# Pooled attention and a mixture of experts: another order of loads, products and copies while the first query tiles are prepared

## The chip, the cores and the metric

The kernel runs on one core of a Trainium2 chip. The metric is the device time of one execution in microseconds (us), as the median over runs. The engines named below are PE (TensorE: products, and transposes as products with an identity), PEld (its weight loads), DVE (VectorE), ACT (ScalarE), POOL (GpSimd) and SP (SyncE). ACT, SP and POOL also issue transfers, each into a queue of its own; those of POOL turn float32 into bf16 on the way where the tiles differ in type. Each engine works through its instructions in the order in which they were written, and waits for semaphores where an operand or a buffer isn't ready.

## The reference

```python
# 8 batches, 8 heads, 576 positions, head size 64
def _attn_ref(q, k, v):
    B, H, S, D = q.shape
    pool = 8
    Sp = S // pool                       # 72
    scale = 1.0 / np.sqrt(D)
    k_p = k.reshape(B, H, Sp, pool, D).mean(axis=3)
    v_p = v.reshape(B, H, Sp, pool, D).mean(axis=3)
    scores = scale * np.matmul(q, k_p.transpose(0, 1, 3, 2))
    scores = scores - np.max(scores, axis=-1, keepdims=True)
    attn = np.exp(scores)
    attn = attn / (np.sum(attn, axis=-1, keepdims=True) + 1e-09)
    return np.matmul(attn, v_p).astype(np.float32)

# x: the attention's output as 4608 tokens of 512; 4 experts, inner size 1024
def _moe_ref(x, domain_probs, w1, w2):
    p = domain_probs / (domain_probs.sum(-1, keepdims=True) + 1e-09)
    out = np.zeros((N, D), dtype=np.float32)
    for e in range(E):
        h = np.maximum(x @ w1[e], 0.0)
        out += p[:, e:e + 1] * (h @ w2[e])
    return out
```

## The kernel before

The 4608 tokens are 36 tiles of 128 (a tile has all 8 heads), and 4 tiles are a group of 512. For each tile the attention runs through a chain: turn the queries (`qT`), `scores`, `maxima` and `less` (subtract the maximum), `expo`, turn the probabilities (`attn_T`), and the context, which ends in `xT`, the group's tokens with the model dimension on partitions. For each group and each expert an up product with `w1` and a relu give `hs`, and a down product with `w2` is collected with the domain's probability into `acc`. The main loop at the end (`for s in range(NSTEP)`, 36 steps of 12 slots) runs the up products of step s + 1 between the down products of step s; the attention of later groups hangs on its slots by `plan`. The order of every engine's work is that of the program text; nothing is rescheduled.

What stands before that loop is written out by hand for the first group, tiles 0 to 3, all of batch 0. Its parts:

- **Loads.** The queries of tile c come by `load_q0(c, queue)` (L138) in float32 into `qf[c]`: tile 0 from ACT, tile 1 from SP, tiles 2 and 3 from POOL. The keys of batch 0 come from SP in three parts into `kf` (L146 a tail, L148 rows 0 to 1 and rows 2 to 3), in front of tile 1's queries; the domain probabilities `dpr` (L154) follow behind them. POOL waits for tile 0's queries by a copy of one element (`waited`, L171), and then issues values, w1 and w2 and tile 2's and 3's queries in the order of L172 to L189.
- **Queries of tiles 0 to 3.** `split_q(c)` casts them to bf16 on ACT (L597), `turn_q0(c)` turns them on PE by 16 products with the identity (L605), `take_q0(c)` copies the result to `qT` on ACT (L613).
- **Keys and values of batch 0.** `fold_keys0` adds each part's 8 rows on DVE (L636, L641), `turn_keys0` turns it on PE (L648), `take_keys0` copies it on DVE (L661). `sum_values0` adds the values on PE (L668), `spread_values0` spreads them on DVE (L677).
- **Tiles 0 and 1.** `sums_by_products` has the sums of the probabilities from PE (L689, then L694 and L696 on DVE); `context_rows` gives the context by rows (L419), scaled on DVE in two halves `x_sb` (L428); `turn_x` turns each half on PE (L703) and copies it to `xT` on ACT (L706). Tiles 2 and 3 use `normalise` and `context` (L449, copy L455).
- **Up product by tile.** `up_tile(s, i, starts)` (L482) runs 16 products for each of two halves of the inner dimension, each half into one PSUM buffer, and behind each a relu on ACT (L486).
- **Idle products.** `idle_products(n)` runs n products of zeros (L622) whose result nobody reads.

PSUM has pools: `ps_h` (two buffers: the up products' outputs, the turned keys, the sums of values, and `xT_ps`), `ps_t` (two: turned queries, turned probabilities, contexts), `ps_o` (two: down products, sums, idle products), `ps_s` (one: scores). A tile in a pool waits until the last reader of the buffer's former tile is done.

`scores(1)` and what comes until the loop over tiles 2 and 3 is the order that the diff edits (bottom of the listing). In it tile 2's cast stands right behind `attn_T(0)`, its turning ahead of `turn_x(0)`, and `scores(3)` behind the whole `down(0, 0)`.

Of the kernel before, what the change touches and what calls it, by code (L numbers as in the profile page):

```python
# [1 line left out]

# [6 lines left out]
ACT = mybir.ActivationFunctionType  # L10
ALU = mybir.AluOpType
AX = mybir.AxisListType
BF16 = mybir.dt.bfloat16
# [4 lines left out]
def kernel(  # L18
# [10 lines left out]
    nc = tc.nc  # L29
# [3 lines left out]
    P = nc.NUM_PARTITIONS  # L33
# [4 lines left out]
    FB = F // P  # L38
# [3 lines left out]
    TPG = G // P  # L42
# [21 lines left out]
    ps_h = ctx.enter_context(tc.tile_pool(name="ps_h", bufs=2, space=PS))  # L64
    ps_o = ctx.enter_context(tc.tile_pool(name="ps_o", bufs=2, space=PS))
    ps_s = ctx.enter_context(tc.tile_pool(name="ps_s", bufs=1, space=PS))
    ps_t = ctx.enter_context(tc.tile_pool(name="ps_t", bufs=2, space=PS))
# [25 lines left out]
    def segments(t0, n):  # L93
        segs = []
        t = t0
        while t < t0 + n:
            b = t // S
            end = min(t0 + n, (b + 1) * S)
            segs.append((b, t - b * S, end - t, t - t0))
            t = end  # L100
        return segs
# [33 lines left out]
    qf = [raw.tile([P, R, D], F32, name=f"qf{c}") for c in range(TPG)]  # L135

    def load_q0(c, queue):
        queue.dma_start(  # L138
            out=qf[c][:].rearrange("p r d -> p (r d)"),
            in_=q[0][:, c * P:(c + 1) * P, :].rearrange("h (c r) d -> c h (r d)", r=R),  # L140
        )
# [5 lines left out]
    for i in (0, 2):  # L147
        nc.sync.dma_start(  # L148
            out=kf[:, i:i + 2, :],
            in_=rows0[i * P:(i + 2) * P].rearrange("(i p) x -> p i x", p=P),  # L150
        )
    load_q0(1, nc.sync)
    dpr = const.tile([NT, P, E], F32, name="dpr")
    nc.sync.dma_start(out=dpr[:], in_=moe_domain_probs.rearrange("(t p) e -> t p e", p=P))  # L154

    still = const.tile([P, G], BF16, name="still")
    nc.vector.memset(still[:], 0.0)  # L157
# [5 lines left out]
    for sign, base in ((1, 0), (-1, SP - 1)):  # L163
        nc.gpsimd.affine_select(
            out=own[:], in_=own[:], compare_op=ALU.is_ge, fill=0.0,
# [159 lines left out]
    def scores(t):  # L325
        sc = ps_s.tile([P, 2, 512], F32, name="sc")
        for b, _, n, at in segments(t * P, P):
            for pair in range(NPAIR):
                nc.tensor.matmul(  # L329
                    sc[at:at + n, pair // 2, (pair % 2) * PW:(pair % 2 + 1) * PW],  # L330
                    lhsT=qT[t][:, pair, at:at + n],
                    rhs=kT[b][:].rearrange("x i p -> x (i p)")[:, pair * PW:(pair + 1) * PW],
                )
        scs[t] = sc
# [6 lines left out]
    def maxima(t):  # L341
        mxs[t] = soft.tile([P, 2, 4], F32, name="mx")
        nc.vector.reduce_max(out=mxs[t][:], in_=by_head(t), axis=AX.X)  # L343

    def less(t):
        st[t] = soft.tile([P, 2, 4, SP], F32, name="d_sb")
        nc.vector.tensor_tensor(  # L347
            out=st[t][:], in0=by_head(t),
            in1=mxs[t][:].unsqueeze(3).to_broadcast([P, 2, 4, SP]), op=ALU.subtract,
        )  # L350

    def less_max(t):
        maxima(t)
        less(t)
# [21 lines left out]
    def sums(t):  # L376
        e = st[t][:]
        if by_dma(t):
            e = attn[t % 2][:, 0:ROWS].rearrange("p (h j) -> p h j", j=SP)
        es = soft.tile([P, H], F32, name="es")  # L380
        nc.vector.reduce_sum(out=es[:], in_=e, axis=AX.X)  # L381
        nc.vector.tensor_scalar_add(out=es[:], in0=es[:], scalar1=1e-9)
        rss[t] = soft.tile([P, H], F32, name="rs")
        nc.vector.reciprocal(out=rss[t][:], in_=es[:])

    def normalise(t):
        sums(t)
        e_sb, rs = st[t], rss[t]
        nc.vector.scalar_tensor_tensor(
            out=attn[t % 2][:, 0:ROWS].rearrange("p (h j) -> p h j", j=SP),  # L390
            in0=e_sb[:], scalar=V_MEAN,
            in1=rs[:].unsqueeze(2).to_broadcast([P, H, SP]),
            op0=ALU.mult, op1=ALU.mult,
        )
# [63 lines left out]
    hs, accs = {}, {}  # L458
# [11 lines left out]
        nc.scalar.activation(out=hs[s][:, fb, :], in_=ps[:], func=ACT.Relu)  # L470


    def up_tile(s, i, starts=tuple(range(0, FB, TPG))):
        g, e = divmod(s, E)
        if s not in hs:
            hs[s] = hpool.tile([P, FB, G], BF16, name="h_sb")
        cols = slice(i * P, (i + 1) * P)
        for f0 in starts:
            ps = ps_h.tile([P, TPG, P], F32, tag="h", name="h_ps")
            for f in range(TPG):  # L480
                for kc in range(KC):
                    nc.tensor.matmul(  # L482
                        ps[:, f], lhsT=w1_sb[e][:, kc, (f0 + f) * P:(f0 + f + 1) * P],
                        rhs=xT[g][:, kc, cols], start=(kc == 0), stop=(kc == KC - 1),
                    )
            nc.scalar.activation(  # L486
                out=hs[s][:, f0:f0 + TPG, cols], in_=ps[:], func=ACT.Relu
            )

    o_ps = {}  # L490

    def down(s, i, f0=0, f1=FB):
        g, e = divmod(s, E)
        t = g * TPG + i
        if f0 == 0:
            o_ps[t] = ps_o.tile([P, DM], F32, name="o_ps")
        ps = o_ps[t]
        for fb in range(f0, f1):
            nc.tensor.matmul(  # L499
                ps[:], lhsT=hs[s][:, fb, i * P:(i + 1) * P], rhs=w2_sb[e][:, fb, :],  # L500
                start=(fb == 0), stop=(fb == FB - 1),
            )
# [76 lines left out]
    for g in range(2, NG):  # L579
        for i in range(TPG):  # L580
            t = g * TPG + i
# [14 lines left out]
    def split_q(c):  # L596
        nc.scalar.copy(out=qrow[c][:], in_=qf[c][:])  # L597


    def turn_q0(c):  # L600
        ps = ps_t.tile([P, R, NC, NPAIR], F32, tag="t", name="qT_ps")
        heads = ident[:].rearrange("x (c a z) -> x c a z", z=2, c=NC)
        for r in range(R):
            for z in range(2):
                nc.tensor.matmul(  # L605
                    ps[z * D:(z + 1) * D, r], lhsT=qrow[c][:, r], rhs=heads[:, :, :, z],
                    start=True, stop=True,
                )
        return ps

    def take_q0(c, ps):
        qT[c] = qtp.tile([P, NPAIR, P], BF16, name="qT")
        nc.scalar.copy(  # L613
            out=qT[c][:].rearrange("x a (c r) -> x a c r", r=R),
            in_=ps[:].rearrange("x r c a -> x a c r"),
        )


    def idle_products(n):
        ps = ps_o.tile([P, DM], F32, name="o_ps")  # L620
        for _ in range(n):
            nc.tensor.matmul(ps[:], lhsT=still[:, 0:P], rhs=still[:], start=True, stop=True)  # L622
# [8 lines left out]
    def fold_keys0(p1, i0, i1):  # L631
        rows = kraw[0][0:p1, i0:i1]
        src = kf[0:p1, i0:i1]
        for n in (4, 2):
            w = n * D
            nc.vector.tensor_add(  # L636
                out=rows[:, :, 0:w], in0=src[:, :, 0:w], in1=src[:, :, w:2 * w]
            )
            src = rows
        twice = [p1, i1 - i0, 2, D]  # L640
        nc.vector.tensor_tensor(  # L641
            out=kpad0[0:p1, i0:i1], in0=rows[:, :, 0:D].unsqueeze(2).to_broadcast(twice),
            in1=rows[:, :, D:2 * D].unsqueeze(2).to_broadcast(twice), op=ALU.add,
        )

    def turn_keys0(p1, i0, i1):
        for i in range(i0, i1):
            nc.tensor.transpose(  # L648
                kT_ps[:, i, 0:p1], kpad0[0:p1, i].rearrange("p z d -> p (z d)"),
                ident[0:p1, 0:p1],  # L650
            )
# [46 lines left out]
    def turn_x(t, halves):  # L698
        n = KC // 2
        for i in range(2):  # L700
            ps = ps_h.tile([P, n, P], BF16, tag="h", name="xT_ps")
            for kc in range(n):
                nc.tensor.transpose(  # L703
                    ps[:, kc], halves[i][:, kc * P:(kc + 1) * P], ident[:]
                )
            nc.scalar.copy(  # L706
                out=xT[0][:, i * n:(i + 1) * n, t * P:(t + 1) * P], in_=ps[:]
            )
        idle_products(1)
# [6 lines left out]
    take_q0(0, turn_q0(0))  # L716
    for part, n in (((TAIL, 4, 5), 3), ((P, 0, 2), 4), ((P, 2, 4), 3)):
        fold_keys0(*part)
        turn_keys0(*part)
        idle_products(n)  # L720
    take_keys0()
# [6 lines left out]
    spread_values0(sum_values0())  # L728
    scores(1)
    attn_T(0)  # L730
    split_q(2)
    maxima(1)
    idle_products(2)
    xT[0] = grp.tile([P, KC, G], BF16, name="xT")
    sums_by_products(0)
    x_sb = context_rows(0, 2)
    pt = turn_probs()
    qT_ps = turn_q0(2)
    idle_products(1)
    turn_x(0, x_sb)  # L740
    less(1)
    expo(1)
    take_q0(2, qT_ps)
    domain_probs(pt)
    up_tile(0, 0, (0,))
    attn_T(1, copy=nc.vector.tensor_copy)
    up_tile(0, 0, (TPG,))
    split_q(3)
    sums_by_products(1)
    x_sb = context_rows(1, 2)  # L750
    scores(2)
    idle_products(1)
    turn_x(1, x_sb)
    less_max(2)
    expo(2)
    up_tile(0, 1, (0,))
    take_q0(3, turn_q0(3))
    up_tile(0, 1, (TPG,))
    down(0, 0)
    scores(3)  # L760
    normalise(2)
    less_max(3)
    collect(0, 0)
# [20 lines left out]
    for s in range(NSTEP):  # L784
        for slot in range(SLOTS):
            part, i = slot % 3, slot // 3
# [41 lines left out]
```

## Time and profile before

| what | value |
|---|---|
| median of 3 runs | 550.18 us (549.75 to 551.51) |
| the profiled execution, its time | 550.72 us |
| the profiled execution, its span (first to last instruction) | 548.6 us |
| PE busy | 538.1 us, 98% of the span |
| ACT, DVE, POOL busy | 213.0, 263.8, 70.7 us |
| first up product of the main loop (L466) starts | 36.58 us |
| mean load on the 16 DMA engines, 18 to 38 us | over 1 (1.28), 204 GB/s |

A line of the timeline or the chain of waits has the start and the length in us, the engine and what ran. A group of instructions shows the output tile, an arrow and the inputs; `x16` is a count. A load's line in the list of issues has the median time from issue to landing, which for one issue is its own time. PE's busy time counts pipelined products, so a busy PE need not be one at its peak. Matmul starts are followed by the next in the array before they end, and the reader of a PSUM tile starts about 0.3 to 0.5 us behind the last product's start. Where a stretch of the span is shown, its columns are busy time and count for each engine, the granted clock of PE, the share of the DMA engines and GB/s.

### The profile page before, as it was taken

How to read it: one execution, taken by the hardware profiler on the slowest of the kernel's cores; microseconds unless marked ns; L12 is line 12 of the kernel's file. 1: busy time of each engine (PE TensorE's matmuls, PEld its weight loads, DVE VectorE, ACT ScalarE, POOL GpSimd, SP SyncE). 2: the span in 40 equal slices, each digit the busy share in tenths (PEclk: the TensorE clock that was granted, in tenths of full speed). 3: DMA queues.
4: the chain of work that ended last, by engine and by line, in shares of the span. 5: the costliest groups of instructions: out<-in, count | busy, mean ns of one | idle time of the engine just before them, and what ended most of it. 6: DMA issues, size and time to landing. Idle time of an engine off the chain costs nothing.

```text
span 548.6 us, 7422 instructions
## 1 busy us (share of the span) xinstructions
PE 538.1 (98%) x2945; PEld 262.7 (48%) x3000; DVE 263.8 (48%) x457; ACT 213.0 (39%) x356; POOL 70.7 (13%) x120
## 2 busy tenths in 40 slices
PE   8899999999999999999999999999999999999997
PEld 3664554444444444444444444444444444444444
DVE  5764847444744446544554444744474444422223
ACT  2554653333333333333333333333333333333330
POOL 6344101121111101012011100101010000000000
PEclk9999999999999999999999999999999999999999
DMA  9999935655646463366535642335333431111002
GB/s 207 219 203 196 201 43 129 83 76 83 124 67 78 77 121 75 49 85 103 99 53 78 81 108 39 54 41 110 51 53 42 85 65 31 23 38 39 0 1 76
DMA packets 110273, 46.43 MB, mean 85 GB/s; under 512 B 87548, under 2 KB 104764, under 8 KB 110240
## 3 DMA queue, kind: packets, MB, share of 16 engines
q0 software_dynamic: 51040, 21.96, 32.3%
q1 hardware_dynamic: 58912, 23.68, 17.9%
q8 instruction: 23, 0.38, 0.3%
q10 hardware_dynamic: 288, 0.33, 0.3%
q14 instruction: 10, 0.08, 0.1%
HBM read 45.16 MB, written 9.44 MB: 100 GB/s over the span
## 4 chain that ended last, share of the span: by engine, by line
PE 95%; DMA 2%; ACT 1%; issue 1%; POOL 1%; DVE 0%
PE o_ps L499 45%; PE h_ps L466 44%; DMA qf<-in_q_dram 2%; PE x_ps L419 2%; PE sc L329 2%; PE h_ps L482 1%; PE x_ps L449 0%; PE at_ps L403 0%; PE o_ps L531 0%; POOL vraw L80 0%; PE qT_ps L319 0%; ACT qrow L597 0%; ACT xT L706 0%; PE qT_ps L605 0%; DVE d_sb L347 0%
## 5 line engine op out<-in xcount | busy, mean ns | idle before, releaser
L470 ACT ACTIVATE h_sb<-h_ps 128x512 bf16<-128x512 f32 x280 | 167.1, 597 | 296.2 <-PE h_ps L466 292.0
L466 PE MATMUL h_ps<-xT,w 128*128 128x512 bf16 x1088 | 271.6, 379 | 1.5
L499 PE MATMUL o_ps<-w,h_sb 128*128 128x512 bf16 x1122 | 268.3, 379 | 1.3
L499 PEld LDWEIGHTS <-h_sb 128*128 128x128 bf16 x1144 | 111.6, 98 | 132.9
L514 DVE SCALAR_TENSOR_TENSOR acc<-o_ps,p_sb,acc 128x512 f32<-128x512 f32 x107 | 80.3, 750 | 179.5 <-PE o_ps L499 176.8
L466 PEld LDWEIGHTS <-w 128*128 128x128 bf16 x1120 | 106.0, 98 | 117.1
L510 DVE TENSOR_SCALAR acc<-o_ps,p_sb 128x512 f32<-128x512 f32 x36 | 27.0, 750 | 61.6 <-PE o_ps L499 61.6
L557 POOL COPY gated<-x_sb0of 1x1 bf16<-1x1 bf16 x28 | 7.8, 278 | 365.5 <-DVE x_sb0of L428 365.5
L108 POOL DMA_DIRECT2D qrow<-in_q_dram x36 | 30.4, 847 | 23.5 <-issue 7.7
L343 DVE TENSOR_REDUCE mx<-sc 128x8 f32<-128x576 f32 x36 | 27.2, 756 | 12.0 <-PE sc L329 12.0
L347 DVE TENSOR_TENSOR d_sb<-sc,mx 128x576 f32<-128x576 f32 x36 | 27.3, 757 | 1.2
L428 DVE SCALAR_TENSOR_TENSOR x_sb0of<-x_ps,rs 128x512 bf16<-128x512 f32 (+1 forms) x30 | 20.2, 674 | 12.4 <-PE x_ps L419 11.7
L360 ACT ACTIVATE attn<-d_sb 128x576 bf16<-128x576 f32 x30 | 20.5, 683 | 3.8 <-DVE d_sb L347 0.6
L381 DVE TENSOR_REDUCE es<-attn 128x8 f32<-128x576 bf16 x28 | 20.8, 744 | 0.0
L419 PEld LDWEIGHTS <-attnT 128*128 128x128 bf16 (+1 forms) x165 | 12.4, 100 | 7.2 <-issue 1.3
L329 PEld LDWEIGHTS <-qT 128*128 128x128 bf16 (+1 forms) x160 | 11.1, 100 | 8.7 <-issue 2.0
L419 PE MATMUL x_ps<-vbd,attnT 128*128 128x192 bf16 (+5 forms) x165 | 15.2, 231 | 0.0
L329 PE MATMUL sc<-kT,qT 128*128 128x144 bf16 (+1 forms) x160 | 15.0, 227 | 0.1
L622 PE MATMUL o_ps<-still 128*128 128x512 bf16 x30 | 10.4, 470 | 1.3 <-DVE still L157 1.3
L244 DVE TENSOR_TENSOR vraw<-vraw 128x1280 bf16<-128x1280 bf16 (+1 forms) x14 | 9.1, 653 | 0.2
L244 DVE TENSOR_TENSOR kraw<-kraw 128x1280 bf16<-128x1280 bf16 (+1 forms) x14 | 9.0, 641 | 0.2
L482 PE MATMUL h_ps<-xT,w 128*128 128x128 bf16 x128 | 8.4, 219 | 0.4 <-ACT xT L455 0.2
(86 smaller groups left out, 153.1 us busy)
## 6 DMA issues: line engine op xcount, KB each, us to landing
out_dram<-acc SPq DMA_DIRECT2D x35, 256.0 KB, 2.0
w<-in_moe_w_dram POOLq DMA_DIRECT2D x10, 512.0 KB, 14.1
kraw<-in_k_dram POOLq DMA_DIRECT2D x7, 512.0 KB, 7.6
qrow<-in_q_dram POOLq DMA_DIRECT2D x28, 128.0 KB, 3.6
vraw<-in_v_dram POOLq DMA_DIRECT2D x7, 512.0 KB, 7.4
w<-in_moe_w_dram POOLq DMA_DIRECT2D x3, 1024.0 KB, 16.2
kf<-in_k_dram SPq DMA_DIRECT2D x2, 512.0 KB, 6.1
vraw<-in_v_dram POOLq DMA_DIRECT2D x2, 256.0 KB, 6.0
```

The source lines that it names most:

```text
L108: nc.gpsimd.dma_start(out=qrow[t][at:at + n], in_=q[b][:, tok:tok + n, :].rearrange("h p d -> p h d"),)
L329: nc.tensor.matmul(sc[at:at + n, pair // 2, (pair % 2) * PW:(pair % 2 + 1) * PW], lhsT=qT[t][:, pair, at:at + n], rhs=kT[b][:].rearrange(" ...
L343: nc.vector.reduce_max(out=mxs[t][:], in_=by_head(t), axis=AX.X)
L347: nc.vector.tensor_tensor(out=st[t][:], in0=by_head(t), in1=mxs[t][:].unsqueeze(3).to_broadcast([P, 2, 4, SP]), op=ALU.subtract,)
L360: nc.scalar.activation(out=attn[t % 2][:, 0:ROWS].rearrange("p (h j) -> p h j", j=SP), in_=st[t][:].rearrange("p g h j -> p (g h) j"), fun ...
L381: nc.vector.reduce_sum(out=es[:], in_=e, axis=AX.X)
L419: nc.tensor.matmul(ps[at:at + n, h0 * D:(h0 + c1 - c0) * D], lhsT=attnT[t][:, i, at:at + n], rhs=flat[:, c0 * D:c1 * D], start=(i == 0), s ...
L466: nc.tensor.matmul(ps[:], lhsT=w1_sb[e][:, kc, fb * P:(fb + 1) * P], rhs=xT[g][:, kc, :], start=(kc == 0), stop=(kc == KC - 1),)
L470: nc.scalar.activation(out=hs[s][:, fb, :], in_=ps[:], func=ACT.Relu)
L499: nc.tensor.matmul(ps[:], lhsT=hs[s][:, fb, i * P:(i + 1) * P], rhs=w2_sb[e][:, fb, :], start=(fb == 0), stop=(fb == FB - 1),)
L510: nc.vector.tensor_scalar_mul(out=accs[t][:], in0=ps[:], scalar1=p_sb[:, e, t:t + 1])
L514: nc.vector.scalar_tensor_tensor(out=accs[t][:], in0=ps[:], scalar=p_sb[:, e, t:t + 1], in1=accs[t][:], op0=ALU.mult, op1=ALU.add,)
```

## The change

Five edits, all ahead of the main loop:

1. Tile 1's queries are no longer loaded right behind the keys. After the second of the three key parts (rows 0 to 1) is folded, DVE sets one element of `qf[1]` to zero, and SP issues the load, which has to wait for that memset; the load of `dpr` goes behind it.
2. `turn_x` takes its PSUM tiles from `ps_t` instead of `ps_h`.
3. Tile 2's cast (`split_q(2)`) goes from behind `attn_T(0)` to behind `expo(1)`, and its turning and copy from both sides of `turn_x(0)` to behind `attn_T(1)`. Two idle products stand ahead of `turn_x(0)` where the turning and one idle product stood.
4. The second half of tile 0's up product goes from behind `attn_T(1)` to behind `scores(2)`, ahead of `turn_x(1)`, where an idle product stood; its relu is held back (`relus`) and comes on ACT behind the copies of `turn_x(1)`. `split_q(3)` goes from ahead of tile 1's sums to behind `expo(2)`.
5. `up_tile(0, 1)` runs in one piece with `turn_q0(3)` behind it instead of between its halves, and `scores(3)` stands between the halves of `down(0, 0)`.

```diff
--- before.py
+++ after.py
@@ -1,5 +1,6 @@
 
 from contextlib import ExitStack
+from functools import partial
 
 import concourse.bass as bass
 import concourse.tile as tile
@@ -149,9 +150,7 @@
             out=kf[:, i:i + 2, :],
             in_=rows0[i * P:(i + 2) * P].rearrange("(i p) x -> p i x", p=P),
         )
-    load_q0(1, nc.sync)
     dpr = const.tile([NT, P, E], F32, name="dpr")
-    nc.sync.dma_start(out=dpr[:], in_=moe_domain_probs.rearrange("(t p) e -> t p e", p=P))
 
     still = const.tile([P, G], BF16, name="still")
     nc.vector.memset(still[:], 0.0)
@@ -470,7 +469,7 @@
         nc.scalar.activation(out=hs[s][:, fb, :], in_=ps[:], func=ACT.Relu)
 
 
-    def up_tile(s, i, starts=tuple(range(0, FB, TPG))):
+    def up_tile(s, i, starts=tuple(range(0, FB, TPG)), relus=None):
         g, e = divmod(s, E)
         if s not in hs:
             hs[s] = hpool.tile([P, FB, G], BF16, name="h_sb")
@@ -483,9 +482,14 @@
                         ps[:, f], lhsT=w1_sb[e][:, kc, (f0 + f) * P:(f0 + f + 1) * P],
                         rhs=xT[g][:, kc, cols], start=(kc == 0), stop=(kc == KC - 1),
                     )
-            nc.scalar.activation(
-                out=hs[s][:, f0:f0 + TPG, cols], in_=ps[:], func=ACT.Relu
-            )
+            relu = partial(
+                nc.scalar.activation,
+                out=hs[s][:, f0:f0 + TPG, cols], in_=ps[:], func=ACT.Relu,
+            )
+            if relus is None:
+                relu()
+            else:
+                relus.append(relu)
 
     o_ps = {}
 
@@ -698,7 +702,7 @@
     def turn_x(t, halves):
         n = KC // 2
         for i in range(2):
-            ps = ps_h.tile([P, n, P], BF16, tag="h", name="xT_ps")
+            ps = ps_t.tile([P, n, P], BF16, tag="t", name="xT_ps")
             for kc in range(n):
                 nc.tensor.transpose(
                     ps[:, kc], halves[i][:, kc * P:(kc + 1) * P], ident[:]
@@ -716,6 +720,13 @@
     take_q0(0, turn_q0(0))
     for part, n in (((TAIL, 4, 5), 3), ((P, 0, 2), 4), ((P, 2, 4), 3)):
         fold_keys0(*part)
+        if part[2] == 2:
+
+            nc.vector.memset(qf[1][0:1, 0, 0:1], 0.0)
+            load_q0(1, nc.sync)
+            nc.sync.dma_start(
+                out=dpr[:], in_=moe_domain_probs.rearrange("(t p) e -> t p e", p=P)
+            )
         turn_keys0(*part)
         idle_products(n)
     take_keys0()
@@ -728,36 +739,36 @@
     spread_values0(sum_values0())
     scores(1)
     attn_T(0)
-    split_q(2)
     maxima(1)
     idle_products(2)
     xT[0] = grp.tile([P, KC, G], BF16, name="xT")
     sums_by_products(0)
     x_sb = context_rows(0, 2)
     pt = turn_probs()
-    qT_ps = turn_q0(2)
-    idle_products(1)
+    idle_products(2)
     turn_x(0, x_sb)
     less(1)
     expo(1)
-    take_q0(2, qT_ps)
+    split_q(2)
     domain_probs(pt)
     up_tile(0, 0, (0,))
     attn_T(1, copy=nc.vector.tensor_copy)
-    up_tile(0, 0, (TPG,))
-    split_q(3)
+    take_q0(2, turn_q0(2))
     sums_by_products(1)
     x_sb = context_rows(1, 2)
     scores(2)
-    idle_products(1)
+    relus = []
+    up_tile(0, 0, (TPG,), relus)
     turn_x(1, x_sb)
+    relus.pop()()
     less_max(2)
     expo(2)
-    up_tile(0, 1, (0,))
+    split_q(3)
+    up_tile(0, 1)
     take_q0(3, turn_q0(3))
-    up_tile(0, 1, (TPG,))
-    down(0, 0)
+    down(0, 0, 0, FB // 2)
     scores(3)
+    down(0, 0, FB // 2, FB)
     normalise(2)
     less_max(3)
     collect(0, 0)
```

## What the change was expected to do

> **What bounds the kernel now.** I read the page's parts 1 and 4, then the stretches of the span, then the chain of waits in order of time, then each load's time from issue to landing, and the timeline for the exact starts.
>
> ```profile
> span 548.6 us, 7422 instructions
> ...
> 0.00:18.00 18.00, 14.20 (x127) 7.33 (x129) 11.33 (x30) 5.86 (x9) 10.39 (x23) 1.00 0.98 216
> 18.00:38.00 20.00, 19.10 (x232) 13.76 (x233) 15.07 (x33) 12.10 (x23) 6.83 (x9) 1.00 1.28 204
> 38.00:540.00 502.00, 499.37 (x2553) 238.41 (x2601) 233.96 (x389) 195.04 (x325) 53.46 (x88) 1.00 0.46 75
> ```
>
> The columns after the stretch and its length are busy time and count of PE, PEld, DVE, ACT and POOL, then clock, DMA share, GB/s. From 38 us on PE is busy 499.37 of 502 us: whatever time the first `up(1, 0)` (L466) is moved by, the end is moved by. All that the diff touches lies before that, so the question is when L466 first starts: 36.58 us.
>
> ```profile
> 8.03 8.47 DMA qf<-in_q_dram
> 16.50 0.02 issue
> 16.53 0.63 ACT qrow L597
> 17.15 0.04 issue
> 17.20 0.44 PE qT_ps L605 x16
> 17.64 0.32 PE o_ps L622
> 17.96 0.13 PE xT_ps L703 x2
> ...
> 27.46 0.77 DVE mx L343
> 28.23 0.02 issue
> 28.25 0.77 DVE d_sb L347
> 29.02 0.02 issue
> 29.04 0.69 ACT e_sb L367
> 29.73 0.48 ACT xT L455
> 30.21 0.04 issue
> 30.25 1.96 PE h_ps L482 x32
> ```
>
> (Start, length, what.) Two links matter. First, tile 2's queries land at 16.50; their cast and turning stand in PE's order ahead of tile 0's `turn_x`, though its operands were ready earlier (`x_sb` halves end 16.60 and 16.93 by the timeline). Second, `scores(3)` ends late, and its maximum, subtraction and exponential hold ACT until the copy of tile 2's context, for which `up_tile(0, 2)` waits until 30.25.
>
> ```profile
> qf<-in_q_dram ACTq DMA_DIRECT2D x1, 256.0 KB, 4.2
> qf<-in_q_dram SPq DMA_DIRECT2D x1, 256.0 KB, 7.2
> ...
> 11.67 0.45 PE L605 MATMUL qT_ps<-ident,qrow 128*64 128x64 bf16 x16
> ```
>
> (Last number of a load: us to landing.) Tile 1's queries, issued at 2.56, land at 9.76, but PE turns them at 11.67, behind `scores(0)`. So they have slack of 11.67 - 9.76 - 0.70 (cast 0.62 and two handoffs of 0.03 and 0.05), 1.2 us.
>
> **Step 1: the later load.** The memset follows DVE's `kpad` of the second key part (7.80 + 0.29 = 8.09); the nearest row, two memsets in 0.12 us (L193), makes it 0.1 us, and SP issues at 8.2. Behind it on SP stands only the `dpr` load (0.84 us to issue); its reader, L222, runs at 15.9, so 6 us cover it. No row shows this load beside a full POOL queue. From below: a 256 KB store on a quiet SP queue lands in 2.0 us; the slowest store in 2.7. From above: tile 0's load with the keys beside it took 4.2; this load itself, queued behind the keys, 7.2. It will stand alone in its queue beside a busy one (in 7.5 to 9.5 us the software queue has a share of 82.4%), so I take the middle between 2.7 and 4.2, 3.4: landing 11.6 (bounds 10.2 and 15.4).
>
> By the Trainium skill, DMA: Bandwidth & Descriptors, section Anatomy of one DMA, a transfer costs about 2.0 us and its bytes over 436 GB/s, fitted for GpSimd's path; an estimate from it for 256 KB is 2.6 us, landing 10.8, and by that step 2 below would cost nothing. The 4.2 us row is the nearer one and speaks for more.
>
> **Step 2: what the load holds up.** Cast, then PE's turn at 11.6 + 0.70 = 12.3 instead of 11.67: 0.63 late. Behind it on PE wait an idle product, the sums of values (1.27), `scores(1)` and `attn_T(0)`; on ACT `take_q0(1)`, `expo(0)` and the copy of tile 0's probabilities. The binding one goes sums of values, DVE's spreading (1.29), maxima (0.75), the sum `es`. Maxima end at 15.54 and `es` starts at 15.65, so about 0.08 of the delay is absorbed there; another 0.20 further on, where the second `xT` copy would wait for ACT's first (0.27 pitch) anyway. 0.63 - 0.28 = **0.35 us lost**.
>
> **Step 3: tile 2's turning behind `attn_T(1)`.** With the load in time, PE has L222 and two idle products until 16.9; the halves of `turn_x` start at 16.92 and 17.03 (the idle products' end; 16.93 + 0.05 for the second half, and 0.05 more for its weights) instead of 17.80 and 17.91. Copies end 17.60 and 17.87, and the up product runs on from 17.92 instead of 18.81: 0.89 earlier. `split_q(2)` stands behind `expo(1)` (to 18.46) and ends at 18.97; `attn_T(1)` is on PE at 18.70, the turning at 19.02 to 19.39. `domain_probs` is off DVE by 18.88, so the copy of `attnT` runs 19.18 to 19.67. PE waits 0.3 us for it, since the half product that filled this gap (0.9 us) is gone; that half now fills the wait for `x_sb` instead (20.44 to 21.33), where before an idle product of 0.22 and 0.37 of waiting stood. Tile 1's `turn_x` starts at 21.33, its copies end 22.02 and 22.28, and the next up product runs from 22.32 instead of 23.13: 0.81 left.
>
> **Step 4: ACT's order and `scores(3)`.** `relu` of the moved half (22.18), `expo(2)` (DVE's subtraction ends 22.75; 22.78 to 23.47), `split_q(3)` to 23.99; its load landed 19.65. PE ends `up_tile(0, 1)` at 23.99 and turns tile 3 at 24.04 to 24.41. `take_q0(3)` waits behind two relus and ends at 25.51. Half of `down(0, 0)` (4 x 0.216) covers PE until 25.27, then 0.29 of waiting, `scores(3)` at 25.56 instead of 27.01, the other half to 26.68. `attn_T(2)` is 0.58 earlier. But now DVE's maxima and subtraction for tile 3 (26.01 to 27.56) are done before ACT is free: attnT copy to 27.91, `expo(3)` 27.82 to 28.51, context copy 28.57 to 29.13 instead of from 29.64. PE goes straight from `down(0, 1)` to `up_tile(0, 2)` at 29.27 instead of 30.25: **0.98 gained**. After that tile 3's stages keep their lengths (DVE's `attn` is ready by 31.0, when PE asks), and L466 starts 0.98 earlier.
>
> **Step 5: what costs nothing.** Idle products: 2+1+1+1+1 before, 2+2+1+1 after. `turn_x` in the other PSUM pool: each tile there takes the buffer of one that was read before (the first halves' are those of `at_ps(0)` and `x_ps(0)`, read at 15.28 and 16.93). Moving 256 KB of loading behind 8.2 us delays the software queue by at most 256 KB at 384 GB/s (the rate of 5 to 7 us), 0.7 us; the tightest reader is the second half of `down(0, 0)`: that part of w2 is issued at 11.22, lands 13.7 later at 24.9, then 25.6, and is wanted at 25.8 + 0.35. Without that margin each us later costs one.
>
> **Sum:** -0.98 + 0.35 = -0.63 us. The profiled execution took 550.72 (548.6 and 2.1 around it), so 550.1; the median of the runs is 0.54 below that, 550.18, so **549.6 us**. Its own range, with landings from 10.9 (2.7 us) to 12.4 (4.2 us): -0.98 to +0.15, 549.2 to 550.3.
>
> **The rivals.**
> - *Tile 1's queries decide the head, slower.* Above 12.2 us of landing the 0.98 is eaten (12.2 + 0.70 - 11.67 - 0.28); beyond, each us costs one. With its old 7.2 us it lands at 15.4: -0.98 + 4.43 - 0.28 = +3.2, 553.4. For it: 7.2 and 8.5 us on other query loads of the same size; against: those were queued behind keys or weights. The 0.3% line is crossed at a landing of 13.9. Chance 0.17, some 0.08 above that line.
> - *The second pair of key parts lands earlier without the query load.* It took 6.8 us against 5.3 for the pair before; with 5.3 keys are there at 7.4 and `scores(0)` is up to 1.5 earlier. But the turn behind it still needs the queries: at best 10.2 + 0.70 = 10.9, 0.77 before the old 11.67, so -0.98 - 0.77 = -1.75, 548.4. Against: the query load was behind the keys in one queue. Chance 0.12.
> - *PE's clock falls.* The wait thins PE's work around 12 us. The stretch 9 to 11 us already has little of it and kept its clock:
>
> ```profile
> 9.00:11.00 2.00, 0.97 (x7) 1.00 1.21 196
> ```
>
>   A 3.4 us stretch with 2.8 us of work at half rate would add up to 2.8: 552.4. The Trainium skill, TensorE: Matmul & The Clock Gate, Part 1, has the clock halved after an idle window of about 3.4 us; the longest gap I work out is under 1.1 us, so by that rule it doesn't happen, and the row agrees. Chance 0.04.
> - *The head's gain is lost at the weights*, w2 landing 1 us later than worked out: 549.9 to 550.5. Chance 0.07.
>
> **The numbers.** The forecast has 0.60. A difference under 0.3% (1.65 us) can't be told from none here: the three runs shown spread by 1.8 us. Faster than that needs the second rival with luck: 0.11. Slower: the late load's tail, the clock, and chance, 0.13. Same 0.76. The range takes in the second rival's 548.4 and the first up to some 14 us of landing, 551.6.
>
> **What would show it.** Tile 1's cast (L597) starting near 11.6 and its turn (L605) near 12.3; tile 2's turn after `at_ps`; `turn_x` before it, from about 17.3; `scores(3)` between two halves of L499; no wait between `down(0, 1)` and `up_tile(0, 2)`; L466 first at about 35.95. A cast later than 12.4, or a `down` half waiting for w2, would make it wrong.

## The result and the profile after

The changed kernel takes 554.39 us (median of 6 runs, 553.5 to 555.99), the kernel before in the same comparison 550.58 (549.75 to 551.81): a ratio of 1.0069, 95% interval 1.0049 to 1.0088. It is slower by some 3.8 us; 549.6, and a range of 548.4 to 551.6, had been forecast. The page of the changed kernel begins so, with PE's granted clock as the last row shown:

```profile
span 552.7 us, 7479 instructions
...
PEclk9799999999999999999999999999999999999999
```

The span is 4.1 us longer than before, and the second slice shows a clock under full speed. In finer stretches (stretch, length, PE's busy time and count, granted clock, DMA share, GB/s):

```profile
10.00:12.00 2.00, 0.54 (x5) 1.00 1.18 179
12.00:14.00 2.00, 0.00 (x0) 0.65 1.13 276
14.00:16.00 2.00, 0.52 (x16) 0.50 1.15 245
16.00:18.00 2.00, 2.00 (x20) 0.50 1.21 267
18.00:20.00 2.00, 2.00 (x16) 0.64 1.21 211
20.00:22.00 2.00, 1.65 (x17) 1.00 1.22 204
```

PE does nothing from 12 to 14 us, and then works at half clock until about 19.5. The timeline of the changed kernel says for what it waits; the last two lines are ACT's cast of tile 1's queries and the first product of the main loop:

```profile
7.91 0.61 SPq L139 DMA_DIRECT2D qf<-in_q_dram  x1
10.20 0.41 PE L328 MATMUL sc<-kT,qT 128*128 128x144 bf16 x4
15.48 0.64 PE L609 MATMUL qT_ps<-ident,qrow 128*64 128x64 bf16 x16 [4.88 <-ACT qrow L601]
16.45 2.34 PE L672 MATMUL v_ps<-vraw,ident 128*128 128x128 bf16 x16
...
14.81 0.62 ACT L601 CAST qrow<-qf 128x512 bf16<-128x512 f32 x1 [7.14 <-DMA qf<-in_q_dram]
...
40.69 5.56 PE L465 MATMUL h_ps<-xT,w 128*128 128x512 bf16 x25
```

Issued at 7.91, tile 1's queries are cast at 14.81, and PE, done with `scores(0)` at 10.61, idles 4.88 us. The sums of values then take 2.34 us for 16 products where they took 1.27. The main loop's first up product comes at 40.69 instead of 36.58, 4.11 later: the whole difference of the spans is made before that line, as the steps had it, though with the other sign. The chain of waits, which had gone through tile 2's queries, now goes through tile 1's load (start, length, what):

```profile
7.57 0.29 DVE kpad L645
7.86 0.05 DVE kraw L640
7.91 6.82 DMA qf<-in_q_dram
14.73 0.02 issue
```

### The profile page after: what moved, and what is told of

Same layout as the page of the kernel before. It is cut to its first block, busy times and chain, and to the rows that moved or that the text cites. A ratio compares the mean times of both kernels' runs of the same rounds, so it can differ in the third digit from the quotient of the medians.

```text
span 552.7 us, 7479 instructions
## 1 busy us (share of the span) xinstructions
PE 542.3 (98%) x3000; PEld 264.3 (48%) x3000; DVE 263.3 (48%) x458; ACT 212.7 (38%) x356; POOL 70.7 (13%) x120
## 4 chain that ended last, share of the span: by engine, by line
PE 96%; DMA 2%; ACT 1%; DVE 0%; issue 0%; SPq 0%; ACTq 0%
PE o_ps L503 45%; PE h_ps L465 44%; PE x_ps L418 2%; PE sc L328 2%; PE h_ps L481 1%; DMA qf<-in_q_dram 1%; DMA kf<-in_k_dram 1%; PE x_ps L448 1%; PE v_ps L672 0%; PE at_ps L402 0%; PE o_ps L535 0%; ACT attnT L403 0%; PE qT_ps L318 0%; PE o_ps L626 0%; DVE kraw L640 0%; PE qT_ps L609 0%
```

## The experiments

Two questions: is the whole loss that of the later load, so that the other edits gain what had been worked out; and why does the load take 6.8 us. All ratios are to the kernel before, measured beside it.

**Edit 1 undone, and edit 1 alone.** e1 is the changed kernel with the early load:

```diff
+    load_q0(1, nc.sync)
     dpr = const.tile([NT, P, E], F32, name="dpr")
+    nc.sync.dma_start(out=dpr[:], in_=moe_domain_probs.rearrange("(t p) e -> t p e", p=P))
...
-        if part[2] == 2:
-
-            nc.vector.memset(qf[1][0:1, 0, 0:1], 0.0)
-            load_q0(1, nc.sync)
-            nc.sync.dma_start(
-                out=dpr[:], in_=moe_domain_probs.rearrange("(t p) e -> t p e", p=P)
-            )
```

> The changed kernel without edit 1: tile 1's queries and dpr are loaded right behind the keys again. Theory A (the whole loss is the later load: its first packet comes 4.2 us after the issue, PE waits 4.9 us and then runs 6.8 us at half clock; the other edits gain about 1 us as worked out): the cast of tile 1 at about 9.8, the clock 1.00 throughout, the first up product of the main loop near 35.6, 1.0 us under the kernel before (0.998). Theory B (the other edits cost something too, or gain nothing): no faster than the kernel before (1.000 or above), first up product at 36.6 or later.

Measured: 549.27 us (8 runs), ratio 0.9969 (0.9956 to 0.9981). The clock stays at 1.00. e1's timeline:

```profile
8.99 0.62 ACT L603 CAST qrow<-qf 128x512 bf16<-128x512 f32 x1 [1.39 <-DMA qf<-in_q_dram]
10.65 0.44 PE L611 MATMUL qT_ps<-ident,qrow 128*64 128x64 bf16 x16
15.93 0.27 PE L709 MATMUL xT_ps<-ident,x_sb0of 128*128 128x128 bf16 x2
18.09 0.44 PE L611 MATMUL qT_ps<-ident,qrow 128*64 128x64 bf16 x16
34.54 1.67 PE L467 MATMUL h_ps<-xT,w 128*128 128x512 bf16 x6
```

From the turn of tile 1's queries to the first product of the main loop it is 34.54 - 10.65 = 23.89 us, against 36.58 - 11.67 = 24.91 before: 1.02 shorter. Theory B falls. In this execution the head is another 1.02 earlier because the second pair of key parts was folded from 7.91 instead of 8.93, with the early load in place.

e2 is the kernel before with the lines of edit 1 alone.

> The kernel before with edit 1 alone. Theory A: the load lands 6 to 7 us after its issue at 7.9, PE waits about 5 us and its clock halves, and since the gain of the other edits is missing the time is above that of the changed kernel: +4.8 us on the kernel before (1.0087). Theory B: below the changed kernel, under +3.8 us (1.0069).

Measured: 555.6 us, ratio 1.0083 (1.0063 to 1.0103), above the changed kernel by 1.2 us as theory A has it, though the two intervals overlap. The load takes 7.4 us there, and PE idles 5.46 us. e2's timeline, with the turns of tile 1 and tile 2 and the first product of the main loop:

```profile
16.03 0.64 PE L603 MATMUL qT_ps<-ident,qrow 128*64 128x64 bf16 x16 [5.46 <-ACT qrow L595]
22.07 0.44 PE L603 MATMUL qT_ps<-ident,qrow 128*64 128x64 bf16 x16
41.44 4.91 PE L464 MATMUL h_ps<-xT,w 128*128 128x512 bf16 x21
```

From the turn of tile 1 to the main loop it is 41.44 - 16.03 = 25.41 us, in the changed kernel 40.69 - 15.48 = 25.21. Beside a late load the other four edits shorten this path by 0.20 us only, not by the 1.02 that they are worth beside an early one: tile 2's queries, for which edit 3 spares the wait, have landed long before e2 turns them at 22.07, and nothing waits for them.

**The wait without the fall of the clock.** e3 keeps the load late and gives PE idle products meanwhile:

```diff
     scores(0)
+    idle_products(20)
     split_q(1)
```

> The changed kernel with 20 idle products (4.3 us of PE) between scores(0) and the turn of tile 1's queries, so that PE is busy while it waits for the load. Theory A (the clock is a cost of its own: the products from 15.5 to 20 us take 2.0 us more than at full rate, 0.6 to 1.2 of it in the sums of values): clock 1.00 throughout, wait unchanged, about 2 us faster than the changed kernel, 1.0035 of the kernel before. Theory C (the half clock is hidden behind DVE and ACT): within 0.5 us of the changed kernel, 1.006 to 1.007.

Measured: 552.46 us, ratio 1.0036 (1.002 to 1.0052), 1.93 us under the changed kernel's median. The clock is 1.00 throughout. In e3's timeline the wait before the turn has shrunk to 0.24 us, and the sums of values have their old length:

```profile
10.29 4.48 PE L626 MATMUL o_ps<-still 128*128 128x512 bf16 x19
15.02 0.44 PE L609 MATMUL qT_ps<-ident,qrow 128*64 128x64 bf16 x16 [0.24 <-ACT qrow L601]
15.62 1.27 PE L672 MATMUL v_ps<-vraw,ident 128*128 128x128 bf16 x16
38.47 7.07 PE L465 MATMUL h_ps<-xT,w 128*128 128x512 bf16 x31
```

From the turn to the main loop it is 38.47 - 15.02 = 23.45 us here and 40.69 - 15.48 = 25.21 in the changed kernel. So the half clock costs 1.76 us of the path, beyond the wait that caused it, and theory C falls.

**The same wait, placed earlier.** In e4 the memset and the load stand behind the first key part:

```diff
-        if part[2] == 2:
+        if part[2] == 5:
```

> The changed kernel with the memset behind the first key part (the tail) instead of the second, so that the load is issued at about 4.6, before POOL's transfers move data (7 us). Theory A (the load was late because POOL's transfers had been handed to the engines before it): it lands by 9.8, PE doesn't wait for it, clock 1.00, time as e1 or up to 1 us better if the second key pair still lands at 7.8: 0.996 to 0.998 of the kernel before. Theory D (a load that SP issues behind a wait takes its 6.8 us whatever stands beside it): it lands at 11.4, tile 1's turn is 0.5 us late or more, and e4 is slower than e1.

Measured: 549.14 us, ratio 0.9964 (0.9952 to 0.9976), the same as e1. Issued at 4.61, the load lands 4.6 us later, in time for the turn at 11.00. It was still behind the keys in SP's queue, and the second key pair was folded from 8.26, so nothing was gained over e1.

**What stands ahead of the load.** e5 moves all of POOL's loads behind tile 1's queries (the copy that POOL waits with reads `qf[1]` instead of `qf[0]`, and the block stands behind the load); e6 leaves the values where they are and moves only the rest. e6's edit, shortened:

```diff
     load_rows(vraw[0], v[0], ((0, 2), (2, 4)))
-    load_w1(0, lambda: load_q0(2, nc.gpsimd))
...
+            again = const.tile([1, 1], F32, name="again")
+            nc.gpsimd.tensor_copy(out=again[:], in_=qf[1][0:1, 0, 0:1])
+            load_w1(0, lambda: load_q0(2, nc.gpsimd))
...
```

> The changed kernel with all of POOL's loads (values, weights, later queries) behind tile 1's queries: POOL waits for tile 1's load instead of tile 0's, so nothing of POOL's moves when SP issues at about 7.8. Theory A (in the changed kernel the load's packets stood behind what POOL had handed to the engines: one packet of the hardware queue in 8.5 to 12 us, 187 in 12 to 14.7): it lands 2.0 to 2.9 us after its issue, at 10 to 10.7. Theory D (SP's issue behind a semaphore costs its 6.8 us by itself): it lands at 14 or later. The whole kernel becomes slower, as values and weights start 3 us or more later; only the landing counts.

> The changed kernel with POOL's loads of values as they are (576 KB, issued from 5 to 7 us), and all others behind tile 1's queries. Theory A: the load's packets begin when the values have moved; those alone take 576 KB at 197 GB/s, 2.9 us from 7 us on, so packets from about 10, landing at 10.7 to 11.7, 3 to 4 us after the issue. Theory G (the engines share evenly between the queues from the first packet on, and it is the rate alone that is short): as e5, 2.0 to 3.0 us. Theory D: 6.8 us again.

e7 issues it from ACT's queue:

```diff
-            load_q0(1, nc.sync)
+            load_q0(1, nc.scalar)
```

> The changed kernel with tile 1's load issued from ACT's queue instead of SP's, behind the same memset. Theory A (what POOL handed over before counts, whichever hardware queue the load is in): landing 6 to 7.5 us after the issue, the clock halved, 554 to 555 us. Theory H (SP's queue holds it up, by the keys before it): landing under 4 us after the issue, clock 1.00, 549 to 551 us.

Measured, each in one execution (556.45 us for e5, 552.45 for e6, 554.48 at a clock of 0.994 for e7; in the first two POOL's loads start later, so that only the landing counts): time from issue to landing (last column), in the lists of issues of e5, e6, the changed kernel and e7:

```profile
qf<-in_q_dram SPq DMA_DIRECT2D x1, 256.0 KB, 3.6
```
```profile
qf<-in_q_dram SPq DMA_DIRECT2D x1, 256.0 KB, 4.4
```
```profile
qf<-in_q_dram SPq DMA_DIRECT2D x1, 256.0 KB, 6.8
```
```profile
qf<-in_q_dram ACTq DMA_DIRECT2D x1, 256.0 KB, 6.9
```

The time grows with what POOL has issued before: nothing, the values, values and weights. The queue that it is issued from makes no difference to the landing (theory H falls), and it is no fixed price of a load behind a wait (theory D falls). Where the time goes is in the packets of the two queues. In the changed kernel from 8.5 to 12 us, and then from 12.2 to 12.8:

```profile
q0 software_dynamic: 648, 0.63, 119.1%
q1 hardware_dynamic: 1, 0.00, 0.2%
```
```profile
q0 software_dynamic: 66, 0.07, 67.5%
q1 hardware_dynamic: 43, 0.09, 43.9%
```

For some 4 us after the issue the engines move POOL's packets and one of SP's; then the two queues go side by side. In e6 SP's packets start in the stretch from 9.8 to 10.4 us (24 of them, beside 108 of the last 122 of the values), in e5 by 9.2, 1.4 us after the issue. So theory A's order holds, and even sharing from the first packet (theory G) doesn't. Of the 3.2 us between 3.6 and 6.8, then, some 2.7 pass before the first packets and the rest beside POOL's. How the time divides varies: in e7 the load's first packets move in the stretch from 10.4 to 11 us (10 of them, beside 81 of POOL's), some 2.8 us after the issue at 7.70, and its last after 13 us, so that the landing is the same. What sets the moment of the first packet stays open. Two of theory A's numbers were off: e5's load took 3.6 us where 2.0 to 2.9 was expected, and e6's 4.4 instead of 3 to 4. Even with nothing of POOL's ahead the load takes longer than a store of its size (2.0).

The Trainium skill, DMA: Bandwidth & Descriptors, section Queues, rings and completion order, says that an engine alternates between the queues that have work, a whole packet of some 9 to 17 descriptors at a time. The trace agrees once SP's packets have begun (43 beside 66). It doesn't show the first 4 us to be an alternation: 648 packets on 16 engines are 40 of POOL's on each before one of SP's. It doesn't rule it out either, since no run here shows whether what the trace counts as a packet (about 2 KB in SP's queue, 1 KB in POOL's) is a packet in that sense.

**Which of the other edits gains.** e8 is e1 with `scores(3)` behind the whole of `down(0, 0)`:

```diff
-    down(0, 0, 0, FB // 2)
+    down(0, 0)
     scores(3)
-    down(0, 0, FB // 2, FB)
```

> The early load (e1) with scores(3) behind the whole of down(0, 0) again. Theory A as I now read my own step 4: PE then has no wait before scores(3), which comes 0.6 us later, and expo(3) and the context's copy follow 0.1 to 0.2 us later: 0.1 to 0.2 us slower than e1, 0.997 of the kernel before. Theory J (the place of scores(3) is what frees the chain through the maximum and exponential of tile 3): 0.8 us slower than e1 or more, 0.9985.

Measured: 549.44 us, ratio 0.9976 (0.9963 to 0.9989), 0.17 us over e1's median, which the intervals can't tell from nothing. In the profiles, from tile 3's turn to `up_tile(0, 2)` takes 28.90 - 23.55 = 5.35 us against 28.23 - 23.14 = 5.09 in e1: 0.26 for the place of `scores(3)`. Theory J falls.

e9 is e1 without edits 2 and 3:

```diff
     attn_T(0)
+    split_q(2)
...
-    idle_products(2)
+    qT_ps = turn_q0(2)
+    idle_products(1)
...
-    split_q(2)
+    take_q0(2, qT_ps)
...
-    take_q0(2, turn_q0(2))
```

with `turn_x` in `ps_h` again.

> The early load (e1) without edits 2 and 3: tile 2's cast and turning stand ahead of turn_x(0) again, with the second half of tile 0's up product, up_tile(0, 1) and scores(3) as in the changed kernel. Theory A (what e1 gains comes mostly from edit 3: tile 0's turn_x no longer waits for tile 2's queries, which land at 16 to 16.5 whatever the keys do): turn_x(0) at 17.3 or later instead of 16.1, and about 0.8 to 1.5 us slower than e1, 0.999 to 1.000 of the kernel before. Theory K (the gain comes from the later rows: up products and scores(3)): within 0.3 us of e1, 0.997.

Measured: 550.92 us, ratio 1.0003 (0.999 to 1.0016): all of e1's gain is gone. Part of this is the clock: five of e9's twelve executions have a mean granted clock of 0.997 or less, none of e1's eight. The other seven have a median of 549.95 us, 0.68 over e1's; theory K falls either way. The places of the loss in e9's timeline:

```profile
15.03 0.62 ACT L603 CAST qrow<-qf 128x512 bf16<-128x512 f32 x1 [1.18 <-DMA qf<-in_q_dram]
16.30 0.28 PE L709 MATMUL xT_ps<-ident,x_sb0of 128*128 128x128 bf16 x2
19.12 0.28 PE L695 MATMUL es_ps<-own,attnT 128*128 128x2 bf16 x5 [0.59 <-DVE attnT L405]
21.47 0.27 PE L709 MATMUL xT_ps<-ident,x_sb1of 128*128 128x128 bf16 x2 [0.46 <-ACT xT L712]
```

`turn_x(0)` starts at 16.30, 0.37 after e1's, not the 1.2 expected, as the queries landed at 15.0 in this execution. But tile 1's turn, too, is earlier there (10.24 against 10.65); counted from it, `turn_x(0)` is 6.06 - 5.28 = 0.78 late. The wait for `attnT`, 0.59 where it is 0.21 in e1, adds nothing to that: in e1 tile 2's turning stands in its place, and `es_ps` comes 8.88 us behind tile 1's turn here and 8.09 there, 0.79 apart. The rest of the loss comes where the second half of tile 1's `turn_x` waits 0.46 for ACT's copy of the first: its PSUM pool is shared with the up products, and edit 4 holds back the relu that would free the other buffer. From `ps_t` it doesn't wait. In the kernel before it doesn't either, where no relu is held back, so that this part is the price of taking edit 2 away from under edit 4. From the turn of tile 1 to the main loop it is 35.34 - 10.24 = 25.10 us, 1.21 more than e1's 23.89, and 0.78 of this is there at `turn_x(0)`.

## Why the prediction was wrong

Its terms, and what the profiles make of them, as lengths of the path up to the main loop's first product:

| step | predicted, us | measured, us | from |
|---|---|---|---|
| other edits (steps 3 and 4) | -0.98 | -1.02 | e1 against before, 23.89 - 24.91 |
| tile 1's turn later (steps 1 and 2) | +0.63 | +3.81 | 15.48 - 11.67 |
| absorbed behind it (step 2) | -0.28 | -0.44 | e3 against e1, 23.45 - 23.89 |
| PE's clock (a rival, left out) | 0 | +1.76 | changed kernel against e3, 25.21 - 23.45 |
| sum | -0.63 | +4.11 | 40.69 - 36.58 |

The last column adds up by construction, as its rows are differences between the same starts in single executions. Two of them need care. The 3.81 has 1.02 us of earlier keys in it: against e1, whose keys came as early as the changed kernel's, the turn is 15.48 - 10.65 = 4.83 later. And the -1.02 was measured beside the early load; e2 shows 0.20 beside the late one, so the sum was wrong to add the gain and the loss as if they were independent.

- **Step 1 failed.** It gave the load 3.4 us, the middle between the slowest store (2.7) and tile 0's load beside the keys (4.2), on the ground that it "will stand alone in its queue beside a busy one". It took 6.8. Alone in its own queue says little: what counts is what the other queue had issued before it (3.6 with nothing, 4.4 with the values, 6.8 with values and weights). The row it set aside, 7.2 us for the same load behind the keys, was put down to its own queue, and was the nearest in number. The issue itself was well placed (7.91, worked out as 8.2).
- **Step 2's mechanism was right, its size followed step 1.** The binding line went from the cast to the turn and to the sums of values, in PE's order, with some 0.4 us absorbed.
- **Step 3 and step 4 hold in sum with the load in time**, 1.02 us against 0.98. Step 3's first stage alone, worked out as 0.89 earlier, is 0.85 from tile 1's turn to `turn_x(0)` (17.80 - 11.67 = 6.13 before, 5.28 in e1). Of the two rows the place of `scores(3)` is the lesser: 0.26 us in e8's profile, near the 0.17 between the 0.81 and the 0.98 worked out. In time e1 gains 0.3% (0.19 to 0.44), about 1.3 us by its medians. Most of what this has beyond the 1.02 goes with the clock: of the 22 executions of the kernel before that were measured with e1, 8 have a mean granted clock of 0.997 and a median of 551.87 us, the other 14 one of 550.37, and against these e1 gains 1.10.
- **Step 5 was right.** Behind the main loop's first product nothing is lost, and no wait for weights appears in the chain.
- **The rival that came true** is the first, tile 1's queries deciding the head. Its price by formula, landing at 14.73, is -0.98 + 3.76 - 0.28 = +2.5; e3, with the wait and without the clock, measures +1.9. It was given 0.17, and its price stood without the third rival, which it brings along.
- **The clock** was given 0.04 on a longest gap "under 1.1 us"; the gap became 4.88. The rows that were to show that little work keeps the clock, 0.97 of 2 us, did not cover the case. Nor did the one profile show that the kernel before loses its clock itself in some executions. Its price, up to 2.8, was of the right size (1.76).
- **The second rival** had the query load hold up the keys. With the late load the second pair was folded from 7.55 to 7.96 us on (six traces), with the early one from 8.93 (before), 8.32 (e8), 7.91 (e1) and 7.50 (e9). The means are 0.43 apart, but the early ones spread by 1.4, so whether the load holds up the keys stays open.

## What to carry to other kernels

A load's time from issue to landing is no property of its size and its queue: price a load that is moved behind other issues by a row in which as many bytes of any queue were issued ahead of it, and ask what stands still until it lands. A wait on PE costs its length and, if it takes enough work out of a few microseconds, a stretch at half clock on top, so the two are one rival with one price. Where a bundle of edits loses, undo them one by one: here four of five were worth 0.3% with the load early, and one move of a load took back three times that. Don't add such pieces up unseen: beside the late load the same four shortened the path by 0.20 us instead of 1.02, as the wait that they spare was gone.

## What the runs showed that was not expected

The clock fell without an idle stretch of its full length. In e6 PE waited 2.45 us, from 10.37 on. The mean clock of 0.85 in the half microsecond up to 12 us puts the fall at 11.85, when PE had idled for 1.48 us; in the 3.42 us before the fall it was busy for 1.71. The clock then stayed at half for 6.82 us, though PE was busy for 5.85 of them. In the changed kernel PE was busy for 1.34 of the 3.41 us before the fall at 12.60. e6's stretches:

```profile
11.50:12.00 0.50, 0.00 (x0) 0.85 0.03 4
8.43:11.85 3.42, 1.71 (x11) 1.00 1.01 207
11.85:18.67 6.82, 5.85 (x54) 0.50 0.71 126
```

The Trainium skill, TensorE: Matmul & The Clock Gate, Part 1, gives an idle window of about 3.4 us as the condition. The length of the window fits; that PE has to be idle through it doesn't, since here half of it was work. The pieces of constant clock in the traces are multiples of 3.41 us long. In stretches of this length, placed as each trace's clock record begins, the full clock was kept with 2.33 of 3.42 us busy in the kernel before (9.24 to 12.66) and with 2.20 of 3.41 in e4 (7.67 to 11.08), so a bound on the busy share would lie between 1.71 and 2.20. The longest gap in e4's stretch was 1.15 us, so a bound on the gap, between 1.15 and 1.48, would fit as well.

The kernel before loses the clock in some of its executions. Its mean granted clock was 0.997 in 8 of the 22 executions measured with e1, 8 of 17 with e5 to e8 and 5 of 17 with e9, and those took 1.1 to 1.5 us longer by the medians. As an estimate, 0.3% of 548 us is 1.6 us lost, some 3.3 us at half clock. Of the 29 executions of e1, e4 and e8 none shows it, of e9's twelve five do (one at 0.994), and e9 differs from e1 only by edits 2 and 3: so keeping the clock goes with these two. In two of the changed kernel's six executions the mean was 0.996 or 0.997 instead of 0.993 or 0.994, and these two were the fastest (553.5 and 553.96 us). No execution at 0.997 was profiled, so where in it the clock fell stays open.

A 256 KB load of queries with nothing of POOL's ahead, and only the 72 KB of `dpr` behind it, takes 3.6 us from issue to landing (e5), where the median store of the kernel before, of the same size, takes 2.0; its first packets move 1.4 us after the issue.
